# Gated sum of full and sliding-window attention: single PSUM banks in the first and last stage, another load order

## The chip, the core and the metric

The kernel runs on one core of a Trainium2 chip. The metric is device time in microseconds (us) of one execution. The core's engines have queues of their own and meet at semaphores: TensorE (PE, with its weight loads as PEld), VectorE (DVE), ScalarE (ACT), GpSimd (POOL) and SyncE (SP), which issues most of the DMA transfers. Sums of matmuls are made in PSUM, which has eight banks; a bank holds 512 fp32 numbers for each of 128 partitions.

## What is computed

Two attentions over the same input x (2048 tokens, width 512, 32 heads of 16), mixed by a gate for each token:

```python
g = sigmoid((x * gate_w).sum(-1, keepdims=True))
# A: full attention, every query with all 2048 keys
p = softmax(einsum("bhqd,bhkd->bhqk", q, k) * 16 ** -0.5)
a = (p @ v) @ wo_A
# B: eight keys per query, at distances 0, 2, ..., 14 behind it
logits = einsum("bhsd,bhswd->bhsw", q, k[idx]) * 16 ** -0.5
b = (softmax(logits masked where idx < 0) @ v[idx]) @ wo_B
out = g * a + (1 - g) * b
```

Here q, k and v are x times the parts of `A_wqkv` or `B_wqkv`. All inputs and the output are bf16.

## The kernel before

Full attention is the bulk: 32 heads x 16 key tiles of 128 x 4 query chunks of 512 gives 2048 score blocks of 128 keys x 512 queries. They are worked off in 32 periods, each of four heads and one query chunk. ScalarE takes the exponential of most blocks, two or three to an instruction, straight out of PSUM (`pT <- ring`). Two PSUM rings take turns: `rA` of three banks and `rB` of two (`act_stream`). The other blocks are done by polynomials on VectorE (`dve_unit`) or GpSimd (`pool_unit`), from two single banks `w0` and `w1`. The last bank is `acc`, where the products of probabilities and values are summed. Attention B runs on GpSimd beside all this, and the projections to q, k, v and the output go through `w0` and `w1`.

The order of instructions is not written out by hand. A planner (`Plan`) runs through generators, each a job that yields steps such as ("pe", priority, planned duration, function) or ("dve", ...), and records the instructions engine by engine in the order in which a plan with those durations would start them. `Chained` ties each engine's instructions to that order, so every operation has line 339, that of its helper. The planned figures decide the order alone; at run time each engine works through its queue and waits for the semaphores that the framework puts in. The framework keeps account of PSUM by tile: two instructions that touch the same tile, even in different banks of it, can be made to wait for each other.

The first stage, before the first exponential, is this. SP starts the loads: `wkr` (the first 128 key columns), then x in four blocks `xr` of 512 tokens, then `wqr`, `wv` and the rest (lines 389 to 400). TensorE turns each block round, 128 x 128 at a time (`x_half`), and the two halves of a block are copied from PSUM to `xT` by VectorE and ScalarE. The blocks use the banks of the rings: blocks 0 and 2 a tile `xt` of three banks in `rA`, blocks 1 and 3 one of two in `rB`. `XARR` and `WARR` are the planned arrivals. From `xT` come the first keys (`k_job` with i = 0): four matmuls for each block into a bank, of which VectorE takes the maximum (`kmax_all`) and ScalarE writes the copy with a bias (`kt_all`). `sel_job` makes `kmax` and `selk_all` from the maxima; `q_job` makes the first queries: four matmuls, `absq` on VectorE, one matmul with `selk_all`, and `qt` on VectorE. The stream begins with the matmuls of `qt` and `kt_all` into the first ring.

The last stage begins when the last exponentials have read the rings. `end_banks` takes both rings once more, as tiles `last` of three and two banks, and hands out their five banks as resource "e". `post_job` of the last period copies `acc` to `accS`, transposes it, divides by the row sums (`rden`, then `otok`); `ot_job` transposes the result to `oT`; `final_job` and `direct_job` multiply it by the output weights `awo`, and `bwo` for attention B. Of the last four output tiles two go through VectorE (`osb`) and two through ScalarE (`osc`), each followed by its DMA. Among the matmuls stand others into `acc` with zero weights: filler, which the planner puts where TensorE would be idle (`fill_pass`; into `heat` before the stream).

Of the kernel before, what the change touches and what calls it, by code (L numbers as in the profile page):

```python
# [51 lines left out]
class Plan:  # L52
# [36 lines left out]
    def advance(self, gen, t, val):  # L89
        while True:  # L90
            try:
                req = gen.send(val)
            except StopIteration:
                return
            val = None
            op = req[0]
            if op == "acq":
                self.seq += 1
                self.reqs[req[1]].append((req[2], self.seq, t, gen))
                return  # L100
            if op == "rel":
                self.slots[req[1]].append((t, req[2]))
                if len(req) > 3:
                    self.held["job"] -= 1
                continue
            if op == "set":
                ev = req[1]
                ev.time = t
                ws, ev.waiters = ev.waiters, []
                for g_ in ws:  # L110
                    self.advance(g_[0], max(t, g_[1]), None)
                continue
            if op == "wait":
                ev = req[1]
                if ev.time is None:
                    ev.waiters.append((gen, t))
                    return
                t = max(t, ev.time)
                continue
            if op == "delay":  # L120
                t += req[1]
                continue
            if op == "now":
                val = t
# [45 lines left out]
    def gate(self, need):  # L170

        if need is None:
            return 0.0
        if need == "e":
            return min((x[0] for x in self.slots["e"]), default=None)
        if not self.slots[need] or self.held["job"] >= self.cap_job:
            return None
        return min(x[0] for x in self.slots[need])
# [43 lines left out]
    def run(self):  # L222
        while True:
# [27 lines left out]
            else:  # L251
# [22 lines left out]
                    self.idle_fill(st, 1 + (x[6] is not None))  # L274
                if x[6] is not None:
                    slot = self.take(x[6], st)
                    self.held["job"] += 1
                    more = x[5](slot)
                else:
                    more = x[5]()  # L280
# [12 lines left out]
def kernel(  # L293
# [22 lines left out]
    const = ctx.enter_context(tc.tile_pool(name="const", bufs=1))  # L316
    work = ctx.enter_context(tc.tile_pool(name="work", bufs=2))
    ps = ctx.enter_context(tc.tile_pool(name="ps", bufs=1, space=PSUM))

    prev_inst = {}  # L320
    dep_info = mybir.DependencyInfo(mybir.DependencyClass.NoSync, mybir.DependencyReason.SCHED_ONLY)
# [62 lines left out]

    a_w3 = A_wqkv.rearrange("(c p) n -> p c n", p=128)
    xr = [work.tile([128, 2, TPC, D], BF16, name="xr", tag=tg, bufs=1) for tg in ("prod", "vsh")]
    SP.dma_start(out=wkr[:, :, 0:128], in_=a_w3[:, :, D:D + 128])
    for sc in range(NC):
        SP.dma_start(out=xr[sc // 2][:, sc % 2],
                     in_=x2d[sc * QW:(sc + 1) * QW, :].rearrange("(t p) n -> p t n", p=128))  # L390
    SP.dma_start(out=wqr[:, :, 0:128], in_=a_w3[:, :, 0:128])
    SP.dma_start(out=wv[:], in_=a_w3[:, :, 2 * D:3 * D])
    SP.dma_start(out=wkr[:, :, 128:D], in_=a_w3[:, :, D + 128:2 * D])
# [47 lines left out]
    P.resource("pd", 4)  # L441
    P.resource("none", 0)
    P.resource("e", 0)
    P.resource("prod", 1)
    P.resource("vsh", 1)
    P.resource("ob", 1)
# [16 lines left out]
    THIN = 0.40  # L463
    KRP = 4
    QRP = 3
    XARR = (5.0, 6.9, 8.8, 10.7)
    WARR = (3.4, 11.2)
    GP = 4
    BB = 3
    BR = 1  # L470

    ends = []

    class Bank:
        def __init__(self, kind="w"):
# [2 lines left out]
        def open(self, slot, shape, dtype=FP32):  # L478
            self.slot = slot
            if self.kind == "w":  # L480
                self.t = wtile(slot, shape, dtype)
                return
            t = ends[slot] if dtype == FP32 else ends[slot].bitcast(dtype)[:, 0:QW]
            if len(shape) == 4:
                t = t.rearrange("p (a b c) -> p a b c", a=shape[1], b=shape[2])
            self.t = t

        def close(self):
            return ("rel", self.kind, self.slot, 1)
# [28 lines left out]
    v_left = [NG * NT]  # L518
    final_left = [TPC] * NC

    xts = {}
    ev_xfree = {0: ev_x[0], 1: ev_x[1], 2: Event()}

    def x_job(sc):
        yield ("delay", XARR[sc])
        if sc >= 2:
            yield ("wait", ev_xfree[sc - 2])
        xt = ps.tile([128, 3 - sc % 2, QW], FP32, tag="rA" if sc % 2 == 0 else "rB", bufs=1, name="xt")
        xts[sc] = xt
        left = [2]  # L530
        for hf in range(2):
            yield ("spawn", x_half(sc, hf, xt, left))

    def x_half(sc, hf, xt, left):
        v = xt[:, hf, :].bitcast(BF16).rearrange("p (c t) -> p c t", c=DC)

        def tr():
            P.thin = 0.16
            for tt in range(2):
                for c in range(DC):  # L540
                    PE.transpose(out=v[:, c, tt * 128:(tt + 1) * 128],
                                 in_=xr[sc // 2][:, sc % 2, 2 * hf + tt, c * 128:(c + 1) * 128], identity=ident[:])
        yield ("pe", 0, 0.70, tr)
        dst = xT[:, :, sc * QW + hf * 256:sc * QW + (hf + 1) * 256]
        if hf == 0:
            yield ("dve", 1, 0.62, lambda: V.tensor_copy(out=dst, in_=v))
        else:
            yield ("act", 0, 1.05, lambda: A.copy(out=dst, in_=v))
        left[0] -= 1
        if left[0] == 0:  # L550
            yield ("set", ev_x[sc])

    def w_job():
        yield ("delay", WARR[0])
        yield ("act", -1, 0.45, lambda: w_part(A.copy, wkp, wkr, 0))
        yield ("set", ev_wk)
        yield ("delay", WARR[1] - WARR[0])
        yield ("act", -1, 0.45, lambda: w_part(A.copy, wqp, wqr, 0))
        yield ("set", ev_wq)

    def k_job(i, sc, rel, prio):
        if rel is not None:
            yield ("wait", rel)
        yield ("wait", ev_wk)
        yield ("wait", ev_x[sc])
        w = Bank()
        ring = i == 0 and sc == 2

        def pe(s=None):
            if ring:  # L570
                w.t = xts[sc][:, 2, :]
            else:
                w.open(s, [128, QW])
# [3 lines left out]
        yield ("pe", prio, 4 * MM + SW, pe) + (() if ring else ("w",))  # L577
        k_left[0] -= 1
        if k_left[0] == 0:
            yield ("set", ev_kdone)  # L580
# [2 lines left out]
        def top(src):  # L583
            V.tensor_reduce(out=kmax_all[:, i, sc:sc + 1], in_=src, axis=AX.X, op=ALU.max, apply_absolute_value=True)
        if i == 0:
            left = [2]
            done = Event()
            yield ("spawn", k_top(prio, lambda: top(w.t[:]), left, done))
            yield ("act", 0, 0.60, lambda: A.activation(out=kt, in_=w.t[:], func=ACT.Identity, bias=kbias[:, 0:1]))
            left[0] -= 1  # L590
            if left[0]:
                yield ("wait", done)
        else:
            yield ("dve", prio, VP + 0.06, lambda: V.tensor_scalar(out=kt, in0=w.t[:], scalar1=kbias[:, 0:1],
                                                                  scalar2=None, op0=ALU.add))
        if ring:
            yield ("set", ev_xfree[sc])
        else:
            yield w.close()
        if i:  # L600
            yield ("dve", prio, VP, lambda: top(kt))
        yield ("set", ev_k[i][sc])

    def k_top(prio, fn, left, done):
        yield ("dve", prio, VP, fn)
        left[0] -= 1
        yield ("set", done)

    def sel_job(i, prio):
        for sc in range(NC):  # L610
# [370 lines left out]
    def act_stream():  # L981
        while front[0] < NP:
# [23 lines left out]
            for p_, us in parts:  # L1006
# [189 lines left out]
    def post_job(p):  # L1196
# [7 lines left out]
        yield ("acq", "accS", p)  # L1204
        if p == NP - 1:
            st["s"] = work.tile([128, QW], FP32, name="accS", tag="accS", bufs=2)
            left, done = [2], Event()
            yield ("spawn", k_top(0, lambda: V.tensor_copy(out=st["s"][:, 0:256], in_=acc[:, 0:256]), left, done))
            yield ("act", -1, 0.42, lambda: A.copy(out=st["s"][:, 256:QW], in_=acc[:, 256:QW]))
            left[0] -= 1  # L1210
# [425 lines left out]
    P.run()  # L1636
    if CFG_DEBUG:
        import os
        import pickle
# [41 lines left out]
```

## Time and profile before

| | |
|---|---|
| median of 4 runs | 858.87 us |
| the runs | 857.09, 858.69, 859.05, 864.69 us |
| the profiled execution | 859.46 us |
| its span (first to last instruction) | 857.7 us |
| mean granted TensorE clock | 0.992 |
| first exponential over a ring starts | 18.97 us |
| last exponential ends | 845.69 us |
| last copy of an output tile ends (`osc`) | 854.83 us |
| GpSimd busy | 734.6 us (86% of the span) |

Times within the profile count from the start of the span. The profile is of one execution, and the time outside its span (859.46 - 857.7 = 1.76 us) is not in it. The page gives for each engine the busy time, for each group of like instructions the count and the mean, and it follows the chain of work that ended last back to its start. In a row such as `pT<-ring`, the tile written stands left of the arrow and the tile read right of it. Three stages of the span are to be kept apart: before the first exponential, the stream of exponentials, and behind it.

### The profile page before, as it was taken

What the parts mean: (1) busy time and instruction counts of PE and PEld (TensorE: products, weight loads), DVE (VectorE), ACT (ScalarE), POOL (GpSimd) and SP (SyncE); (2) the same over time, 40 slices, a digit from 0 to 9 for tenths busy, and PEclk for the clock granted to TensorE, in tenths of its full rate; (3) what the DMA queues carried; (4) which work ended last, traced back from release to release, by engine and by line L of the source; (5) the groups of instructions that cost most, each with busy time, mean ns of one, the idle gap of its engine ahead of it and who ended that gap; (6) DMA issues with size and microseconds to landing.
All of it is one profiled execution on the core that took longest, in us unless ns stands there. A gap on an engine that the chain in (4) does not pass through costs nothing.

```text
span 857.7 us, 16082 instructions
## 1 busy us (share of the span) xinstructions
PE 754.5 (88%) x6044; PEld 270.9 (32%) x6044; DVE 748.0 (87%) x1313; ACT 833.2 (97%) x754; POOL 734.6 (86%) x740
## 2 busy tenths in 40 slices
PE   8999999888898898888889899988888999888896
PEld 4333343332333322333333233332332332232332
DVE  4588989899999989989999988899889998999885
ACT  5999999999999999999999999999999999999995
POOL 2586798999899989898999998989999998978970
PEclk9999999999999979999999999999999999999999
DMA  9002133312323232121031304213003203010000
GB/s 295 3 2 71 66 130 111 118 63 75 117 63 117 92 105 69 55 63 50 8 111 32 111 32 135 75 56 112 1 14 117 74 20 124 19 50 7 1 2 26
DMA packets 55711, 59.79 MB, mean 70 GB/s; under 512 B 3648, under 2 KB 52288, under 8 KB 55632
## 3 DMA queue, kind: packets, MB, share of 16 engines
q1 hardware_dynamic: 54816, 58.50, 21.3%
q8 instruction: 47, 0.77, 0.4%
q10 hardware_dynamic: 816, 0.26, 0.1%
q14 instruction: 32, 0.26, 0.1%
HBM read 46.14 MB, written 12.62 MB: 69 GB/s over the span
## 4 chain that ended last, share of the span: by engine, by line
ACT 65%; issue 21%; PE 11%; DVE 2%; DMA 1%; SPq 0%; ACTq 0%
ACT pT L339 64%; PE w L339 3%; PE ring L339 3%; PE acc L339 3%; DVE ta L339 1%; ACT lg L339 1%; PE last L339 1%; DMA xr<-in_A_x_dram 1%; PE xt L339 0%; ACT xT L339 0%; DVE kmax_pk L339 0%; DVE xT L339 0%; DVE kpk L339 0%; DVE pd L339 0%; ACT osc L339 0%
## 5 line engine op out<-in xcount | busy, mean ns | idle before, releaser
L339 ACT ACTIVATE pT<-ring 128x1536 bf16<-128x1536 f32 x722 | 821.9, 1385 | 7.3 <-PE ring L339 3.8
L339 PE MATMUL ring<-qt,kt_all 32*128 32x512 bf16 x1849 | 288.4, 383 | 89.5 <-ACT pT L339 74.7
L339 DVE SCALAR_TENSOR_TENSOR ta<-ta,w 128x512 f32<-128x512 f32 x450 | 301.7, 681 | 6.5
L339 POOL TENSOR_TENSOR prod<-prod 128x512 f32<-128x512 f32 (+1 forms) x208 | 240.3, 1166 | 6.0
L339 PE MATMUL acc<-pT,vp_all 128*17 128x512 bf16 x1804 | 225.8, 385 | 0.1
L339 PEld LDWEIGHTS <-kt_all 32*128 32x128 bf16 x2093 | 111.5, 91 | 331.3 <-issue 315.0
L339 DVE TENSOR_SCALAR ta<-w 128x512 f32<-128x512 uint16 x225 | 153.4, 685 | 40.4 <-PE w L339 37.9
L339 PE MATMUL acc<-ident,z 128*32 128x512 bf16 (+4 forms) x745 | 166.2, 338 | 2.4 <-DVE accS L339 2.0
L339 DVE SCALAR_TENSOR_TENSOR pd<-ta,w 128x512 uint16<-128x512 f32 x225 | 151.5, 677 | 1.8
L339 POOL TENSOR_TENSOR prod<-ksh,qb 128x512 f32<-128x512 bf16 x128 | 145.0, 1156 | 2.4
L339 POOL TENSOR_TENSOR prod<-vsh,lg 128x512 f32<-128x512 bf16 x128 | 136.7, 1099 | 2.5
L339 PE MATMUL w<-qt,kt_all 32*128 32x512 bf16 x244 | 92.5, 385 | 0.2 <-DVE pd L339 0.2
L339 PE MATMUL acc<-pd,vp_all 128*17 128x512 bf16 x244 | 78.8, 381 | 0.0
L339 PEld LDWEIGHTS <-z 128*32 128x32 bf16 x775 | 51.8, 95 | 73.7 <-issue 54.0
L339 POOL TENSOR_TENSOR psc<-psc 128x512 f32<-128x512 f32 x57 | 68.0, 1194 | 4.4
L339 PEld LDWEIGHTS <-vp_all 128*17 128x17 bf16 x2048 | 42.4, 88 | 85.3 <-issue 83.1
L339 POOL TENSOR_SCALAR psc<-psc 128x512 f32<-128x512 uint16 (+1 forms) x38 | 23.5, 618 | 39.9 <-DVE psc L339 32.1
L339 PE MATMUL w<-bw,xT 128*128 128x512 bf16 x192 | 49.6, 381 | 0.4
L339 PEld LDWEIGHTS <-xT 128*128 128x128 bf16 x512 | 30.8, 97 | 29.6 <-issue 16.7
L339 POOL TENSOR_TENSOR lg<-lg,mx 128x256 f32<-128x256 f32 x16 | 10.1, 629 | 25.1 <-DVE mx L339 22.8
L339 DVE CAST kvs<-w 128x512 bf16<-128x512 f32 x32 | 21.8, 682 | 3.8 <-PE w L339 3.7
L339 DVE COPY accS<-acc 128x512 f32<-128x512 f32 (+1 forms) x32 | 21.6, 676 | 2.7 <-ACT accS L339 2.0
(115 smaller groups left out, 493.1 us busy)
## 6 DMA issues: line engine op xcount, KB each, us to landing
ksh<-kv_scr SPq DMA_DIRECT2D x16, 1024.0 KB
vsh<-kv_scr SPq DMA_DIRECT2D x16, 1024.0 KB
kv_scr<-kvs SPq DMA_DIRECT2D x16, 256.0 KB
kt_all<-k_scr SPq DMA_DIRECT2D x6, 512.0 KB
q_scr<-qpk SPq DMA_DIRECT2D x24, 128.0 KB
qt<-q_scr SPq DMA_DIRECT2D x24, 128.0 KB
xr<-in_A_x_dram SPq DMA_DIRECT2D x4, 512.0 KB
out_dram<-osb SPq DMA_DIRECT2D x14, 128.0 KB
```

The costliest lines, as they stand in the source:

```text
L339: return chain_on(self._key, f(*a, **k))
```

## The change

The first and the last stage get PSUM tiles of one bank each. In the first stage a pool `ps0` gives five of them, resource "s", to the transposes of x (half a block each) and to the first key matmuls. When the first ring is wanted, that pool is closed and pools for `rA` and `rB` are opened in its place; when the last exponential has read them both, these are closed and a pool of five single tiles "e" is opened. The loads of x and the first of `wkr` are issued by SP and ScalarE; x block 3 goes in two parts. A table says which engine copies which half of `xT`: VectorE has five halves and ScalarE three. For the first keys the copy is a step behind the maximum, and no longer beside it. In the last `post_job` ScalarE copies the first half of `acc` and VectorE the second. The planned arrivals and some planned durations are other numbers, which shifts the recorded order in the first stage and in the last; `held` counts the "w" banks alone.

```diff
-                if len(req) > 3:
+                if len(req) > 3 and req[1] == "w":
                     self.held["job"] -= 1
...
-        if need == "e":
-            return min((x[0] for x in self.slots["e"]), default=None)
+        if need in ("e", "s"):
+            return min((x[0] for x in self.slots[need]), default=None)
...
-                    self.held["job"] += 1
+                    self.held["job"] += x[6] == "w"
...
+    phase = ExitStack()
+    pools = {"s": phase.enter_context(tc.tile_pool(name="ps0", bufs=1, space=PSUM, reuse_waits="tile"))}
+
+    def next_phase(*names):
+        phase.close()
+        for nm in names:
+            pools[nm] = phase.enter_context(tc.tile_pool(name=f"ps{nm}", bufs=1, space=PSUM, reuse_waits="tile"))
...
-    SP.dma_start(out=wkr[:, :, 0:128], in_=a_w3[:, :, D:D + 128])
-    for sc in range(NC):
-        SP.dma_start(out=xr[sc // 2][:, sc % 2],
-                     in_=x2d[sc * QW:(sc + 1) * QW, :].rearrange("(t p) n -> p t n", p=128))
+    def load_x(t0, n):
+        SP.dma_start(out=xr[t0 // 8][:, t0 // 4 % 2, t0 % 4:t0 % 4 + n],
+                     in_=x2d[t0 * 128:(t0 + n) * 128, :].rearrange("(t p) n -> p t n", p=128))
+    A.dma_start(out=wkr[:, :, 0:128], in_=a_w3[:, :, D:D + 128])
+    load_x(0, 4)
+    load_x(4, 4)
+    load_x(8, 4)
+    load_x(12, 2)
+    load_x(14, 2)
...
+    P.resource("s", 5)
...
-    XARR = (5.0, 6.9, 8.8, 10.7)
-    WARR = (3.4, 11.2)
+    XDVE = ((1, 0), (1, 0), (1, 1), (0, 1))
+    XARR = ((5.8, 5.8), (7.2, 7.2), (8.7, 8.7), (9.4, 10.2))
+    WARR = (4.8, 11.3)
...
-                return
-            t = ends[slot] if dtype == FP32 else ends[slot].bitcast(dtype)[:, 0:QW]
-            if len(shape) == 4:
-                t = t.rearrange("p (a b c) -> p a b c", a=shape[1], b=shape[2])
-            self.t = t
+            else:
+                self.t = pools[self.kind].tile(shape, dtype, tag=f"{self.kind}{slot}", bufs=1, name=f"{self.kind}{slot}")
...
     def x_job(sc):
-        yield ("delay", XARR[sc])
-        if sc >= 2:
-            yield ("wait", ev_xfree[sc - 2])
-        xt = ps.tile([128, 3 - sc % 2, QW], FP32, tag="rA" if sc % 2 == 0 else "rB", bufs=1, name="xt")
-        xts[sc] = xt
         left = [2]
         for hf in range(2):
-            yield ("spawn", x_half(sc, hf, xt, left))
+            yield ("spawn", x_half(sc, hf, left))
...
-        yield ("pe", 0, 0.70, tr)
+        yield ("pe", 0, 0.45, tr, "s")
         dst = xT[:, :, sc * QW + hf * 256:sc * QW + (hf + 1) * 256]
-        if hf == 0:
-            yield ("dve", 1, 0.62, lambda: V.tensor_copy(out=dst, in_=v))
+        if XDVE[sc][hf]:
+            yield ("dve", 1, 0.70, lambda: V.tensor_copy(out=dst, in_=w.t[:]))
         else:
-            yield ("act", 0, 1.05, lambda: A.copy(out=dst, in_=v))
+            yield ("act", 0, 1.02, lambda: A.copy(out=dst, in_=w.t[:]))
+        yield w.close()
...
-        w = Bank()
-        ring = i == 0 and sc == 2
+        w = Bank("s" if i == 0 else "w")
...
         if i == 0:
-            left = [2]
-            done = Event()
-            yield ("spawn", k_top(prio, lambda: top(w.t[:]), left, done))
-            yield ("act", 0, 0.60, lambda: A.activation(out=kt, in_=w.t[:], func=ACT.Identity, bias=kbias[:, 0:1]))
-            left[0] -= 1
-            if left[0]:
-                yield ("wait", done)
+            yield ("dve", prio, VP + 0.09, lambda: top(w.t[:]))
+            yield ("act", 0.5, 0.69, lambda: A.activation(out=kt, in_=w.t[:], func=ACT.Identity, bias=kbias[:, 0:1]))
...
-            ring = ps.tile([128, 3 if k % 2 == 0 else 2, QW], FP32, tag=rname, bufs=1, name="ring")
+            if k == 0:
+                next_phase("rA", "rB")
+            ring = pools[rname].tile([128, 3 if k % 2 == 0 else 2, QW], FP32, tag=rname, bufs=1, name="ring")
...
-        yield ("spawn", end_banks("rA", 3))
-        yield ("spawn", end_banks("rB", 2))
-
-    def end_banks(rname, n):
-
-        yield ("acq", rname, 9)
-        t = ps.tile([128, n, QW], FP32, tag=rname, bufs=1, name="last")
+        yield ("acq", "rA", 9)
+        yield ("acq", "rB", 9)
         now = yield ("now",)
-        for k in range(n):
-            ends.append(t[:, k, :])
-            P.slots["e"].append((now, len(ends) - 1))
+        next_phase("e")
+        P.slots["e"] += [(now, n) for n in range(5)]
...
-            left, done = [2], Event()
-            yield ("spawn", k_top(0, lambda: V.tensor_copy(out=st["s"][:, 0:256], in_=acc[:, 0:256]), left, done))
-            yield ("act", -1, 0.42, lambda: A.copy(out=st["s"][:, 256:QW], in_=acc[:, 256:QW]))
-            left[0] -= 1
-            if left[0]:
-                yield ("wait", done)
+            yield ("act", -1, 0.40, lambda: A.copy(out=st["s"][:, 0:256], in_=acc[:, 0:256]))
+            yield ("dve", 0, 0.42, lambda: V.tensor_copy(out=st["s"][:, 256:QW], in_=acc[:, 256:QW]))
...
-    P.spawn(w_job())
+    P.spawn(w_job(0, wkp, wkr, ev_wk))
+    P.spawn(w_job(1, wqp, wqr, ev_wq))
```

More of the change, by code (lines that the diff above doesn't have):

```diff
@@ L470 @@
     BR = 1
-    ends = []
     class Bank:
@@ L519, with x_half, tr @@
     final_left = [TPC] * NC
-    xts = {}
-    ev_xfree = {0: ev_x[0], 1: ev_x[1], 2: Event()}
     def x_job(sc):
-        yield ("delay", XARR[sc])
-        if sc >= 2:
-            yield ("wait", ev_xfree[sc - 2])
-        xt = ps.tile([128, 3 - sc % 2, QW], FP32, tag="rA" if sc % 2 == 0 else "rB", bufs=1, name="xt")
-        xts[sc] = xt
         left = [2]
         for hf in range(2):
-            yield ("spawn", x_half(sc, hf, xt, left))
-    def x_half(sc, hf, xt, left):
-        v = xt[:, hf, :].bitcast(BF16).rearrange("p (c t) -> p c t", c=DC)
-        def tr():
+            yield ("spawn", x_half(sc, hf, left))
+    def x_half(sc, hf, left):
+        yield ("delay", XARR[sc][hf])
+        w = Bank("s")
+        def tr(s):
             P.thin = 0.16
+            w.open(s, [128, DC, 256], BF16)
             for tt in range(2):
                 for c in range(DC):
-                    PE.transpose(out=v[:, c, tt * 128:(tt + 1) * 128],
+                    PE.transpose(out=w.t[:, c, tt * 128:(tt + 1) * 128],
                                  in_=xr[sc // 2][:, sc % 2, 2 * hf + tt, c * 128:(c + 1) * 128], identity=ident[:])
-        yield ("pe", 0, 0.70, tr)
+        yield ("pe", 0, 0.45, tr, "s")
         dst = xT[:, :, sc * QW + hf * 256:sc * QW + (hf + 1) * 256]
-        if hf == 0:
-            yield ("dve", 1, 0.62, lambda: V.tensor_copy(out=dst, in_=v))
-        else:
-            yield ("act", 0, 1.05, lambda: A.copy(out=dst, in_=v))
+        if XDVE[sc][hf]:
+            yield ("dve", 1, 0.70, lambda: V.tensor_copy(out=dst, in_=w.t[:]))
+        else:
+            yield ("act", 0, 1.02, lambda: A.copy(out=dst, in_=w.t[:]))
+        yield w.close()
         left[0] -= 1
@@ L551, in x_half, with w_job @@
             yield ("set", ev_x[sc])
[L553 to L559, printed above, removed]
+    def w_job(n, dst, src, ev):
+        yield ("delay", WARR[n])
+        yield ("act", -1, 0.45, lambda: w_part(A.copy, dst, src, 0))
+        yield ("set", ev)
     def k_job(i, sc, rel, prio):
@@ L565, in k_job, with pe @@
         yield ("wait", ev_x[sc])
-        w = Bank()
-        ring = i == 0 and sc == 2
[L569 to L573, printed above, removed]
+        w = Bank("s" if i == 0 else "w")
+        def pe(s):
+            w.open(s, [128, QW])
             for c in range(DC):
@@ L576, in pe @@
                    c == 0, c == DC - 1)
-        yield ("pe", prio, 4 * MM + SW, pe) + (() if ring else ("w",))
+        yield ("pe", prio, 4 * MM + SW, pe, w.kind)
         k_left[0] -= 1
@@ L595, in k_job @@
                                                                   scalar2=None, op0=ALU.add))
[L596 to L599, printed above, removed]
+        yield w.close()
         if i:
@@ L602, in k_job @@
         yield ("set", ev_k[i][sc])
-    def k_top(prio, fn, left, done):
-        yield ("dve", prio, VP, fn)
-        left[0] -= 1
-        yield ("set", done)
     def sel_job(i, prio):
@@ L1206, in post_job @@
             st["s"] = work.tile([128, QW], FP32, name="accS", tag="accS", bufs=2)
-            left, done = [2], Event()
-            yield ("spawn", k_top(0, lambda: V.tensor_copy(out=st["s"][:, 0:256], in_=acc[:, 0:256]), left, done))
-            yield ("act", -1, 0.42, lambda: A.copy(out=st["s"][:, 256:QW], in_=acc[:, 256:QW]))
-            left[0] -= 1
-            if left[0]:
-                yield ("wait", done)
+            yield ("act", -1, 0.40, lambda: A.copy(out=st["s"][:, 0:256], in_=acc[:, 0:256]))
+            yield ("dve", 0, 0.42, lambda: V.tensor_copy(out=st["s"][:, 256:QW], in_=acc[:, 256:QW]))
         else:
@@ L1636 @@
     P.run()
+    phase.close()
     if CFG_DEBUG:
```

## The prediction

> **What bounds the kernel now.** I read the page's busy table and its costliest group first, then the chain that ended last at both ends of the span, and last the windows around the one dip in the page's clock row.
>
> ```profile
> PE 754.5 (88%) x6044; PEld 270.9 (32%) x6044; DVE 748.0 (87%) x1313; ACT 833.2 (97%) x754; POOL 734.6 (86%) x740
> L339 ACT ACTIVATE pT<-ring 128x1536 bf16<-128x1536 f32 x722 | 821.9, 1385 | 7.3 <-PE ring L339 3.8
> ```
>
> ScalarE is busy for 97% of the span, and 821.9 us of it are the 722 exponentials over the score rings. They run from 18.97 to 845.69 us. So there are three pieces: 18.97 us before the first exponential, 826.7 us of stream, and 12.0 us behind the last one (857.7 - 845.69). Only 4.8 us of the stream are not exponentials (826.7 - 821.9).
>
> The chain of waits before the stream (start, length, what):
>
> ```profile
> 1.22 4.60 DMA xr<-in_A_x_dram
> ...
> 12.49 1.02 PE xt L339 x4
> 13.52 1.81 PE w L339 x8
> ...
> 15.35 0.69 ACT kt_all L339
> ...
> 16.07 0.70 DVE kmax_all L339
> ```
>
> Look at the last two rows. VectorE's maximum over the fourth key block starts only when ScalarE's copy of the same bank has ended. They are two readers of one bank, one after the other, and the maximum stands second. Earlier in the timeline the order is the other way round and costs as much: ScalarE's first `xT` copy begins at 7.69, after VectorE's copy of the other half of the same `xt` tile (6.97 to 7.66), although it needs other data.
>
> The same chain behind the stream:
>
> ```profile
> 846.86 1.85 PE last L339 x9
> ...
> 848.73 0.18 DVE rden L339
> ...
> 848.96 0.61 PE last L339 x2
> ...
> 849.59 0.43 DVE otok L339
> ...
> 850.07 0.83 PE last L339 x6
> ...
> 850.92 0.43 DVE oT L339
> ...
> 851.40 1.05 PE last L339 x4
> ...
> 852.48 0.70 DVE osb L339
> ...
> 853.20 0.59 ACT osc L339
> ...
> 853.83 0.39 PE last L339
> ...
> 854.25 0.58 ACT osc L339
> ```
>
> Here TensorE and VectorE alternate on a tile named `last`. `rden` starts at 848.73, 0.03 us after a projection matmul into another bank of that tile ends, though its transposes ended at 848.48. `otok` waits for two such matmuls, then two more wait for `otok`, and the second `osc` matmul waits for the first `osc` copy. None of these pairs shares data. They share a tile.
>
> **The change, part by part.** In the changed program's order of instructions, what differs stands before the first ring or behind the last one. The exponentials (722), the polynomial blocks on VectorE and GpSimd, and their order in between are the same, and so are their waits but for the numbering of DMA semaphores. So I give the stream 826.7 us as before, and work out the two ends.
>
> *Start.* The x landings first. Timeline: the first transposes start at 5.86, the second pair at 7.33, both released by a DMA. From the bytes on SP's queue in 0.4 us windows I get when each block's data had moved: 5.1 and 6.5 us for blocks 0 and 1, so 0.75 us from there to the landing. The same count gives 8.0 for block 2, 8.8 for the first half of block 3 and 9.5 for the rest: landings (estimates) at 8.8, 9.5 and 10.3.
>
> [...] Row: SP issues wkr at 0.72 for 0.44 us and the x blocks from 1.22. [...] By the trace the engines are 25 to 40% busy from 2.8 to 3.6 us while the gate vector's 528 tiny packets trickle in, so an earlier issue could fill that, but those packets also move 0.45 us later, behind wkr on ScalarE's queue, into block 0 or 1. Bounds for the landings: 0.5 us earlier, 0.5 us later. I take none. The wkr copy into wkp may then come 1 to 2 us later than 3.95 (it shares with x); it is first needed by a matmul at about 8.2, which covers it. ScalarE's table load slips by one 0.48 us issue, inside its 1.23 us wait for wkr. Splitting x block 3 adds one issue of about 0.5 us on SP; wqr, queued behind it, starts as before, since SP lost the 0.5 us of wkr. wv's issue gains a wait for wkr, which has landed by then; wv is first used after the first ring.
>
> Now the steps with the trace's durations: 8 transposes 0.45 to issue and 0.62 to finish, a VectorE `xT` copy 0.69, a ScalarE one 1.01, four key matmuls 1.02 (0.88 to the next group), maximum 0.69, key copy 0.69.
> - Block 0 at 5.86: VectorE starts half a at 6.52, ScalarE half b at 6.97 (7.69 before), done 7.98. Key block 0 can run at about 8.25 (8.76 before), behind block 1's transposes.
> - Block 2 transposes from 9.1, ends 10.2. VectorE: maximum 0 at 9.3 to 9.97, block 2 copies 10.0 to 11.39. Block 3's second half starts on TensorE when it lands, 10.33, and is copied by VectorE at 11.4 to 12.09. ScalarE: key copy 0 behind its maximum (10.0 to 10.7), block 3 half a to 11.7, wqp to 12.1.
> - TensorE then runs keys 1, 2, 3 and the query: 10.88, 11.76, 12.64, 13.52, ending 14.54. Key 3 needs the copies of 12.09: met. The query needs wqp, 12.1: met by 1.4 us.
> - VectorE: maximum 3 from 13.7 to 14.4, then absq 14.58 to 15.27, kmax, selk to 15.75 (17.25 before), selection matmul to 16.19, qt to 16.98, ring at 17.03, and 0.44 us later (18.53 to 18.97 before) the first exponential at 17.47.
>
> ScalarE's key copies now follow the maxima; the last ends at about 15.1, 2.4 us ahead of that. Without this cover each 0.69 us copy would count. Start: 18.97 - 17.47 = 1.5 us gained; 1.0 to 2.0 with the landings' bounds.
>
> *End.* Take the last exponential's end, 845.69, as fixed.
> - Two projection matmuls stood ahead of the last score-times-value matmuls (845.73 and 846.25). They go behind. [...] acc is done at 846.36, not 846.87: 0.5 gained.
> - accS: ScalarE 846.42 to 846.79, VectorE to 847.25, in this order as before. But six projection matmuls (not four) now stand ahead of its transposes: 846.28 + 6 x 0.22 = 847.60. Transposes to 848.26 (848.48 before); 0.3 of the 0.5 is given back.
> - rden no longer waits for the projection: 848.30; reciprocal; otok 848.78 to 849.20. The five projections between issue by 849.15, just hidden. Otok's transposes 849.25 to 849.64 (850.50 to 850.89 before), oT to 850.10.
> - Last four products: 850.15, 850.37, 850.59, then the remaining pair, the end of which no longer waits for a copy. VectorE 850.57 to 851.94 for two outputs; ScalarE 851.0 to 852.2 for the other two (854.83 before).
> - The last DMA goes as before: 857.7 - 854.83 = 2.9 us behind the last copy.
>
> End: 854.83 - 852.2 = 2.6 us gained.
>
> *Sum.* 1.5 + 2.6 = 4.1 us. Span 857.7 - 4.1 = 853.6; the profiled execution 859.46 - 4.1 = 855.4. That execution is 0.6 us above the median of the runs, 858.87; the forecast is for a median: 858.87 - 4.1 = 854.8, 0.48% less.
>
> **The rivals.**
>
> *Only the end is gained (0.13).* The landings decide the start: TensorE runs without a gap from block 3's landing to the query, so each us that it is late moves the first exponential by one. At 1.5 us late (11.8) the start gains nothing: 858.87 - 2.6 = 856.3. For it: wkr and 528 small packets now share the engines with x, not ahead of it. Against: the bytes ahead of x's end are the same, and the engines move 0.35 MB/us from 4 us on.
>
> *Tiles that stay tied (0.08).* The change doesn't do what it says: single banks still wait for one another, say because two engines reading banks beside each other are held apart. Then only the order at the end is worth something, 0.2 us, and the start perhaps 1: 857.7. Against: the new order lists no VectorE or ScalarE wait for the projection matmuls.
>
> *Clock dips in the stream, slower (0.05).* The price is in the trace (busy of PE, PEld, DVE, ACT, POOL, then the clock):
>
> ```profile
> 305.00:308.00 3.00, 2.89 (x18) 0.71 (x19) 2.50 (x5) 2.88 (x4) 2.86 (x3) 0.50 0.71 209
> 308.00:311.00 3.00, 3.00 (x16) 0.36 (x12) 3.00 (x6) 2.46 (x3) 2.19 (x3) 0.50 1.04 322
> 311.00:314.00 3.00, 3.00 (x18) 1.20 (x17) 0.89 (x2) 2.41 (x3) 2.60 (x3) 0.50 0.65 212
> 314.00:317.00 3.00, 3.00 (x21) 0.89 (x20) 2.69 (x8) 2.86 (x4) 2.58 (x3) 0.81 0.00 0
> ```
>
> TensorE runs at half clock from 305 to 315.2 us, and ScalarE, with 2.76 in the next window, loses 15 - 13.37 = 1.6 us. [...] Against: one dip in 826.7 us, and four runs of before within 2 us but for one of 864.69.
>
> **How the numbers follow.** Both ends gained: 0.74, 854.8, with its own range 852.8 to 856.6 (landings 0.5 each way, one dip more or fewer, 0.4 for hand-over times). The rivals take 856.3, 857.7 and 859.6. For 8 in 10: 852.3 to 857.2. A measurement of this kernel tells about 1% (8.6 us) from no change, so all these cases lie within it. Faster by over 1% (850.3) would need twice the sum: 0.03. Slower by over 1% needs eight dips, or a stall in the stream that I don't see: 0.03. Within: 0.94.
>
> **What would show it.** First exponential near 17.5 us and not behind a key copy; `xT` copies of the two engines overlapping; maxima ahead of key copies; the stretch from the last exponential to the end near 9.4 us, with `rden` released by its own transposes and the last two outputs' copies side by side on VectorE and ScalarE; the stream 826.7 us give or take one dip. It is wrong if the stream's length moves by more than 2 us, if block 3 lands after 11, or if the end keeps alternating.

## The result, and the profile after

| | before | after |
|---|---|---|
| median | 859.8 us (63 runs, 857.09 to 866.68) | 857.44 us (44 runs, 853.86 to 862.85) |
| ratio after to before | | 0.997, 95% interval 0.9959 to 0.9982 |
| the profiled execution, and its span | 859.46, 857.7 us | 858.64, 856.9 us |
| first exponential | 18.97 us | 17.74 us |
| from the last exponential's end to the last `osc` copy's end | 8.66 us | 6.34 us |
| from the last exponential's end to the end of the span | 11.5 us | 9.4 us |

The change is a small gain, 0.3%. It is the sign that was forecast and about 0.6 of the forecast size, and the median lies 0.24 us above the range of 852.3 to 857.2. Two of the page's rows after, and its clock row (tenths of full speed in 40 slices):

```profile
PE 756.3 (88%) x6045; PEld 271.3 (32%) x6045; DVE 749.5 (87%) x1314; ACT 832.1 (97%) x753; POOL 734.6 (86%) x740
PEclk9699999999999999999999999999999999999999
L347 ACT ACTIVATE pT<-ring 128x1536 bf16<-128x1536 f32 x722 | 821.9, 1389 | 9.2 <-PE ring L347 5.9
```

The same 722 exponentials take the same 821.9 us, but ScalarE waits 9.2 us ahead of them (7.3 before). The 6 in the second slice of the clock row, 21 to 43 us, says where to look. Here are the windows of that stretch in the kernel after (start and end, length; busy us and count of PE, PEld, DVE, ACT, POOL; clock; DMA share, GB/s):

```profile
26.00:30.00 4.00, 3.66 (x49) 1.70 (x48) 0.69 (x1) 4.00 (x5) 0.85 (x2) 0.92 0.02 4
30.00:34.00 4.00, 4.00 (x31) 1.12 (x29) 0.69 (x1) 2.89 (x3) 3.75 (x4) 0.50 0.00 0
34.00:38.00 4.00, 4.00 (x34) 1.03 (x33) 2.77 (x5) 2.75 (x5) 3.58 (x6) 0.50 0.00 0
38.00:42.00 4.00, 4.00 (x18) 0.76 (x16) 3.35 (x5) 2.98 (x3) 2.65 (x3) 0.50 0.00 0
42.00:46.00 4.00, 4.00 (x24) 1.14 (x23) 3.17 (x6) 2.96 (x4) 0.00 (x0) 0.87 0.02 4
```

and the same windows before:

```profile
26.00:30.00 4.00, 3.54 (x47) 1.51 (x43) 1.18 (x2) 4.00 (x5) 0.00 (x0) 1.00 0.02 4
30.00:34.00 4.00, 4.00 (x52) 1.72 (x51) 0.91 (x2) 4.00 (x4) 3.44 (x4) 1.00 0.00 0
34.00:38.00 4.00, 3.69 (x43) 1.45 (x42) 3.72 (x8) 4.00 (x6) 3.65 (x5) 1.00 0.00 0
38.00:42.00 4.00, 3.91 (x29) 1.11 (x27) 3.93 (x8) 4.00 (x4) 3.69 (x4) 1.00 0.02 4
42.00:46.00 4.00, 4.00 (x35) 1.14 (x32) 3.92 (x7) 3.88 (x5) 1.33 (x3) 1.00 0.00 0
```

TensorE's granted clock is 0.50 from 29.35 us for 13.65 us. It is then busy without a break and still too slow, and ScalarE falls from 4.00 to less than 3 busy us in each 4. From 26 to 46 us it does 15.58 us of work, against 19.88 before: 4.3 us less. The profiled execution before had the one such stretch of its stream elsewhere, from 304.91 us for 10.24 us. Line the two streams up, exponential by exponential, each counted from its first: up to 29 us they agree to 0.02 us. Then the kernel after falls 4.8 us behind within its stretch, keeps that distance to 0.03 us up to 305 us, and gets 2.3 us of it back where the kernel before has its own. From 330 us to the end nothing more changes.

*The start after*, in the chain of waits (start, length, what):

```profile
3.28 7.52 DMA xr<-in_A_x_dram
...
10.85 3.21 PE s L347 x20
14.06 0.88 PE w L347 x4
...
14.96 0.69 DVE absq L347
...
15.75 0.26 DVE selk_all L347
...
17.74 2.37 ACT pT L347 x2
```

`kmax_all` and `kt_all` are gone from the chain: `absq`, not the last maximum behind ScalarE's copy, is what `selk_all` waits for. TensorE goes from block 3's transposes through three key groups to the query without a break. Block 3's second half, though, begins at 10.84, where 10.33 was forecast. Block 3's transposes end at 11.47 us (12.43 before), and the first exponential comes 6.27 us behind them (6.54 before): 0.96 us of the start's gain lies ahead of that point and 0.27 behind it.

*The end.* First the timeline before, for a point that I had read wrongly (start, length, then engine, line, operation):

```profile
837.35 8.82 ACT L339 ACTIVATE pT<-ring 128x1536 bf16<-128x1536 f32 x8
```

The last exponential, of one bank, ends at 837.35 + 8.82 = 846.17 us. The 845.69 of the table of before and of the prediction is where the chain of waits turns to TensorE: the end of the one before it. After:

```profile
838.59 8.82 ACT L347 ACTIVATE pT<-ring 128x1536 bf16<-128x1536 f32 x8
...
847.47 0.58 PE L347 MATMUL acc<-pd,vp_all 128*17 128x512 bf16 x2
...
849.29 0.60 PE L347 MATMUL e<-identf,accS 128*128 128x128 f32 x4
...
849.93 0.17 DVE L347 TENSOR_TENSOR rden<-e,d 128x16 f32<-128x16 f32 x1 [0.97 <-PE e L347]
...
850.42 0.42 DVE L347 TENSOR_TENSOR otok<-e,rden 128x256 bf16<-128x256 f32 x1
...
851.34 0.42 DVE L347 COPY oT<-e 128x512 bf16<-128x512 bf16 x1 [0.49 <-PE e L347]
...
852.25 1.29 DVE L347 TENSOR_TENSOR osb<-e,fpart 128x512 bf16<-128x512 f32 x2 [0.48 <-PE e L347]
...
852.68 1.07 ACT L347 CAST osc<-e 128x512 bf16<-128x512 f32 x2 [4.18 <-PE e L347]
```

The last exponential ends at 847.41, acc is done 0.64 us later, `rden` starts 0.04 us behind its own transposes (849.89), `otok` waits for no matmul, and the two `osc` copies follow each other beside VectorE's two `osb`. The alternation is gone.

Taken together, from these two executions: start 18.97 - 17.74 = 1.23 us, end 11.51 - 9.44 = 2.07 us (with the spans to the hundredth, 857.68 and 856.85), 3.3 us gained outside the stream. The stream took 827.2 us before (18.97 to 846.17) and 829.7 after (17.74 to 847.41), 2.5 us back. So the change's own part shows, and most of it is hidden in this pair by the two half-clock stretches (4.8 and 2.3 us), in a stream whose instructions were not changed.

### The profile page after: what moved, and what is told of

Same layout as the page of the kernel before. It is cut to its first block, busy times and chain, and to the rows that moved or that the text cites. A ratio compares the mean times of both kernels' runs of the same rounds, so it can differ in the third digit from the quotient of the medians.

```text
span 856.9 us, 16085 instructions
## 1 busy us (share of the span) xinstructions
PE 756.3 (88%) x6045; PEld 271.3 (32%) x6045; DVE 749.5 (87%) x1314; ACT 832.1 (97%) x753; POOL 734.6 (86%) x740
## 4 chain that ended last, share of the span: by engine, by line
ACT 66%; issue 21%; PE 9%; DVE 2%; DMA 1%; SPq 0%; ACTq 0%
ACT pT L347 65%; PE w L347 3%; PE ring L347 3%; PE acc L347 3%; ACT lg L347 1%; DVE ta L347 1%; DMA xr<-in_A_x_dram 1%; PE e L347 0%; PE s L347 0%; SPq L347 0%; DVE kmax_pk L347 0%; DVE absq L347 0%; DVE kpk L347 0%; DVE pd L347 0%; DVE crow L347 0%
## 5 line engine op out<-in xcount | busy, mean ns | idle before, releaser
L347 ACT ACTIVATE pT<-ring 128x1536 bf16<-128x1536 f32 x722 | 821.9, 1389 | 9.2 <-PE ring L347 5.9
```

What stands on the lines that cost most here:

```text
L347: return chain_on(self._key, f(*a, **k))
```

## Experiments

Two theories for the stream. **L** (luck): half-clock stretches are drawn anew in each execution, alike in both kernels, and blur a gain of 3.3 us or more. **E** (early): the earlier start draws them in, so that they are a cost of the change. A third, **G**, is about the start: the gate vector's load, put behind `wkr` on ScalarE's queue, slows x.

### Both kernels again, and each end of the change alone

`start_only` is the kernel after with the end of the kernel before, `end_only` the reverse. All instructions between are the same in the four. The edit of `start_only`:

```diff
-        yield ("acq", "rA", 9)
-        yield ("acq", "rB", 9)
-        now = yield ("now",)
-        next_phase("e")
-        P.slots["e"] += [(now, n) for n in range(5)]
+        yield ("spawn", end_banks("rA", 3))
+        yield ("spawn", end_banks("rB", 2))
...
+        t = pools[rname].tile([128, n, QW], FP32, tag=rname, bufs=1, name="last")
```

with `Bank` and the copies of `acc` as before; `end_only` has the removed lines put in the kernel before, with the pools that they need.

> The kernel before, unchanged. All theories: first exponential at 19.0 us, 12.0 us from the last exponential to the end. [...]

> The changed kernel, unchanged. First exponential at 17.7, 9.5 us behind the last one, so 3.7 us less outside the stream than before. Theory L: the median, too, is 3.7 us less than that of the kernel before measured beside it, about 0.996. Theory E: about 2.3 us less, with a half-clock stretch between 25 and 45 us in the profile again and a lower mean clock than the kernel before.

> The first stage of the changed kernel, the last stage of the kernel before. First exponential at 17.7, 12.0 us behind the last. Theory L: median 1.2 us less than before (0.9986). Theory E: no gain or a loss (0 to 1.5 us more), since the stretches of half clock come with the start.

> The last stage of the changed kernel, the first stage of the kernel before. First exponential at 19.0, 9.5 us behind the last. Both theories: median 2.5 us less than before (0.9971). If it is much less, the gain at the end isn't there in most executions and neither theory holds.

| | median (runs) | ratio to before beside it | first exponential | last exponential to last `osc` end |
|---|---|---|---|---|
| same_before | 861.78 (12) | 0.9989 (0.9965 to 1.0012) | 19.34 | 8.66 |
| same_after | 858.73 (12) | 0.9952 (0.9926 to 0.9978) | 17.77 | 6.34 |
| start_only | 857.29 (12) | 0.9961 (0.9937 to 0.9985) | 17.77 | 8.66 |
| end_only | 858.09 (11) | 0.9958 (0.9939 to 0.9977) | 18.95 | 6.34 |

The last two columns repeat to 0.03 us and are additive, but for the start before (18.95 to 19.34), which follows TensorE's warm-up: in all three profiles with the old start the first exponential comes 13.1 us behind the first transposes. (The 12.0 us of the expectations counts from 845.69; from the true end it is 11.5.) The medians are not additive: each end alone seems to gain as much as both, and the ratio of `start_only` lies below what either theory gave it. Half-clock time decides this. Each execution comes with its mean granted clock, and the time follows it:

```text
granted clock (+-0.001)   before, mean us (runs)   after, mean us (runs)
0.997                     858.50 (14)              854.80 (6)
0.993                     859.68 (17)              856.59 (13)
0.990                     861.86 (16)              858.49 (23)
all                       861.33 (86)              857.89 (56)
mean granted clock        0.9907                   0.9908
straight line             856.95 + 0.47 per 0.001  853.26 + 0.50 per 0.001
```

(before: the 12 runs of `same_before` and the runs of the kernel before made beside all timed experiments; after: the 44 first ones and `same_after`.) At equal clock the kernels are 3.1 to 3.7 us apart, and the lines' ends at full clock 3.7. Each end alone is additive in this measure: held to the line of the kernel before at their own mean clocks (0.9924 and 0.9928), `start_only` gains 1.9 us in the mean and `end_only` 2.1, the whole change 3.4. A dozen runs sample the clock badly: six of the twelve of `start_only` lie within 0.06 us of one another, at 0.995, and its median is one of them.

The mean clock is the same in both kernels, and `start_only`, which has the new start, has no lower one than the kernel before beside it (0.9924 against 0.9903). So theory E is not supported as an explanation of the median. L fits: the mean execution of either loses some 4.5 us to half clock (0.0092 x 0.47 to 0.50 per 0.001), more than the change gains, and the two profiles that I compared happened to differ by 2.5. One gap remains. The 63 first runs of the kernel before have no clock on record. On its line their mean, 860.34, would belong to 0.9928, against the 0.9909 of the 44 runs of the kernel after beside them. So in that comparison the kernel after may have had more half-clock time, worth some 0.9 us (an estimate from the line), and why is open.

What E said of the place is not refuted. `after` has its stretch from 29.35 to 43.0 us, and `same_after` has one there, too: its clock is 0.94 from 26 to 30 us, 0.50 from 30 to 42 and 0.86 from 42 to 46. `before` has 1.00 in all of these windows. Whether the new start makes this one stretch more frequent, and another less, would take many profiles of each.

### Filling TensorE so that the clock holds

That half clock comes where TensorE has little to do was a guess of mine, and is not shown: in the 4 us ahead of the stretch of `after` (25.35 to 29.35) TensorE is busy for 3.54 us with 49 matmuls, and in the same 4 us of the stream of `before` (26.60 to 30.60) for 3.54 us with 49, too, with no half clock behind them. To try it I raised the planner's threshold for filler, in both kernels.

```diff
-    THIN = 0.40
+    THIN = 0.55
```

> The kernel before with one planner constant raised (THIN 0.40 to 0.55), so that more zero-weight matmuls go where TensorE's streaming share of the last 3.4 us falls under 0.55. [...]

> The changed kernel with the same constant. Theory L: clock 0.997 or more, runs close together near 853.5 to 854.5, and 3.6 us (3.2 to 4.0) below the filled kernel before in the median: the gain of both ends, whole. Theory E (the earlier start draws in half-clock stretches, so that the gain is truly 2.4): no more than 2.6 us below it. No stretch at 29 us.

> The changed kernel with the constant at 0.60: 16% more filler than unchanged. Theory L: no stretch in the stream at all; 853.5 to 855, where anything above 854 is the price of TensorE's time for the filler. If filler delays the rings more than it keeps the clock: above 856.

> The changed kernel with the constant at 0.55 and gaps of TensorE filled up to a share of 0.85 (0.70 before). Theory L: as the filled changed kernel, 853.5 to 855. If filling gaps costs the riders on VectorE their place: above 856.

Medians: before_filled 872.19 (6 runs), after_filled 871.18 (6), after_filled_more 872.94 (5), after_filled_share 864.41 (12). The three filled kernels after miss the times that theory L gave; the last two expectations had said above 856 for filler that costs time. The clock was held only in `after_filled_more`: 0.998 to 1.000 in its five runs, 872.7 to 874.0, so its 16% more filler costs 19 us over the 853.3 of the kernel after at full clock. `after_filled_share` has 0.996 in the median and costs 9 us at full clock. These kernels are planned anew from the first extra filler on, so that the price holds for the new order and the filler together. The pair of filled kernels differs by 1.0 us with half-clock time in both: it does not tell L from E.

The last try puts the higher threshold in the first 45 us alone:

```diff
-                        and P.have(P.now + dur) < THIN * P.HAM):
+                        and P.have(P.now + dur) < (0.55 if P.now < 45.0 else THIN) * P.HAM):
```

> The changed kernel with the filler constant at 0.55 for the first 45 us of the plan alone, where both profiles of it had a half-clock stretch of 13.7 us that cost 5. The order behind that point shifts a little. Theory L: no stretch near 29 us, the cluster of runs near 858.7 gone, runs without stretches at 853.5 to 854.5, median 855.5 to 857.5 against 857.4 to 858.7 unchanged. If the filler costs as much as the stretch: 858 or more.

861.0 us (12 runs), ratio to before 1.0003 (0.9982 to 1.0024). A stretch of 13.65 us is gone from its profile: a mean clock of 0.997 over 859.2 us leaves some 5 us at 0.50 (an estimate, 2 x 0.003 x 859.2). But `key_back_3` (0.996) and `gate_last_3` (0.993), with the unchanged filler, have no room for it, either (7 and 12 us). The median clock is 0.9975, and five runs at full clock lie at 859.6 to 860.0. So the clock is better and the floor 6 us worse, as the expectation had it for filler that costs as much as the stretch. Half-clock stretches are cheaper than this way of avoiding them.

### What orders the maxima and the copies

`copies_beside` lets the planner put the first key copies where it did before:

```diff
-            yield ("dve", prio, VP + 0.09, lambda: top(w.t[:]))
-            yield ("act", 0.5, 0.69, lambda: A.activation(out=kt, in_=w.t[:], func=ACT.Identity, bias=kbias[:, 0:1]))
+            left = [2]
+            done = Event()
+            yield ("spawn", k_top(prio, lambda: top(w.t[:]), left, done))
+            yield ("act", 0, 0.60, lambda: A.activation(out=kt, in_=w.t[:], func=ACT.Identity, bias=kbias[:, 0:1]))
...
```

> The changed kernel, with each first key copy free to stand ahead of its maximum, as before. In the recorded order the maxima of the last two blocks then wait for ScalarE's copies. First exponential 0.4 to 0.8 us later than 17.7 (18.1 to 18.5) if that order carries the gain of the start; 17.6 to 17.8 if the single banks alone carry it.

One run, 860.49 us; first exponential 18.60. In its timeline two maxima stand together behind ScalarE:

```profile
13.34 1.84 ACT L347 ACTIVATE kt_all<-s,kbias 128x512 bf16<-128x512 f32 x3 [0.75 <-DVE kmax_all L347]
...
14.64 1.29 DVE L347 TENSOR_REDUCE kmax_all<-s 128x1 f32<-128x512 f32 x2 [1.33 <-ACT kt_all L347]
```

VectorE idles 1.33 us until ScalarE's copies let it in: the wait that the chain of before ended in, back again with single banks. TensorE's first transposes were late in this run, too (6.28 us). So count from the end of block 3's transposes: the first exponential comes 6.89 us behind it here (11.71 to 18.60), and 6.27 us in `after` and in the six runs of the next section. By this one run 0.6 us is the order's, within the 0.4 to 0.8 that was expected; 18.5 was passed by 0.1 for the late start.

### Whose packets delay x

The DMA answers for 5.6 to 6.4 us, after and then before (packets, volume; by queue: packets, MB, share of 16 engines):

```profile
DMA packets 391, 0.14 MB, mean 177 GB/s; under 512 B 253, under 2 KB 391, under 8 KB 391
...
q1 hardware_dynamic: 150, 0.14, 53.3%
q10 hardware_dynamic: 241, 0.00, 17.8%
```

```profile
DMA packets 272, 0.27 MB, mean 343 GB/s; under 512 B 4, under 2 KB 272, under 8 KB 272
...
q1 hardware_dynamic: 272, 0.27, 115.7%
```

q10 is ScalarE's queue. Its 241 packets here are the gate vector's, 2 bytes each. While they run, from 5.2 to 7.5 us, x gets half of its pace (177 GB/s against 343); the same program without them (`gate_load_last` below) moves 350 GB/s from 5 to 6 us and 342 from 6 to 7, where `after` has 287 and 125. Before, they ran at 2.4 to 4.0 us, when little else did (112 GB/s in all). Two edits: the gate vector's load last, on SP; or `wkr` back on SP ahead of x, with the gate vector first on ScalarE's queue.

```diff
-        A.dma_start(out=gw[:], in_=gate_w.rearrange("(c p) -> p c", p=128))
...
+        SP.dma_start(out=gw[:], in_=gate_w.rearrange("(c p) -> p c", p=128))
```

```diff
-    A.dma_start(out=wkr[:, :, 0:128], in_=a_w3[:, :, D:D + 128])
+    SP.dma_start(out=wkr[:, :, 0:128], in_=a_w3[:, :, D:D + 128])
```

> The changed kernel, with the gate vector's load issued by SP behind all other loads. Theory G (its 512 packets of 2 bytes, now in the middle of x, halve the transfers from 5.6 to 7.2 us): the last x packets end near 9.4 us, not 10.3; the transposes of block 3 start at 10.0, not 10.8; first exponential at 16.9 (16.7 to 17.1), not 17.7; all else the same, so 0.8 us off the time at equal clock. Rival (x's pace is set by the bytes alone): first exponential at 17.6 to 17.8.

> The changed kernel, with the first key weights' load back on SP ahead of x and the gate vector first on ScalarE's queue, as before. Theory G: the 2-byte packets go by from 2.5 to 4 us again, while the engines have little else; x ends at 9.8 and the first exponential starts at 17.2 (17.0 to 17.4): the load on two queues cost 0.5 us. If it brought its 0.5 us of issue time: 18.2.

The first run of the former missed: first exponential at 18.09. Its timeline says why:

```profile
1.44 4.91 PE L347 MATMUL heat<-ident,z 128*32 128x512 bf16 x12 [1.44 <-DVE wkp L347]
...
6.28 1.46 PE L347 MATMUL s<-ident,xr 128*128 128x128 bf16 x16
```

TensorE's twelve warm-up matmuls, one each 0.43 us, occupy it until 6.28, and the first transposes take 1.46 us instead of 1.07, though x is there. In the kernel after they ended in time for transposes at 5.91. Here they stand 0.43 us apart to the last: their weight loads come at 4.38, 4.81, 5.24 and 5.66. In `after` the spacing turns from 0.43 to 0.22 us at 5.46 us, where the trace's clock record begins, and in `before` it turns at 4.54, where that record begins: up to that point the matmuls take twice the time, as at half clock. The warm-up, no row of my chain, is a bound of the first stage. Further runs of both edits:

> The gate vector's load last, a second look at the start. In the first look the warm-up matmuls ended late (transposes from 6.28, at half clock), so the landings did not decide. If the first transposes start before 6.0 here: first exponential at 17.3 to 17.5 if the earlier x counts (theory G, held to what TensorE's queue leaves of it), 17.7 to 17.8 if it doesn't.

> As the second look at the gate vector's load last: 17.3 to 17.5 where the first transposes start before 6.0 (theory G), about 18.1 where they start at 6.2 or later, as in the first look.

> The first key load back on SP, a second look. Theory G: block 2 and 3 transposes without a gap (1.96 us for 32) and the first exponential at 17.4 to 17.5 again, 0.3 less than with two queues. Else 17.7 or more.

> As the second look at the key load back on SP: 17.4 to 17.5 by theory G.

| | first transposes | blocks 2 and 3 (32 transposes) take | first exponential |
|---|---|---|---|
| after | 5.91 | 2.21 | 17.74 |
| same_after | 5.97 | 2.18 | 17.77 |
| start_only | 5.34 | 2.18 | 17.77 |
| gate_last_2 | 5.87 | 1.95 | 17.29 |
| key_load_back | 5.99 | 1.96 | 17.47 |
| key_back_2 | 6.28 | 1.95 | 17.69 |
| key_back_3 | 6.29, slow (16 in 1.28 us) | 1.95 | 17.91 |
| gate_load_last, gate_last_3 | 6.28, slow (16 in 1.46, 1.48 us) | 1.95 | 18.09, 18.11 |

Where x no longer has a gap (1.95), the first exponential comes 11.4 us behind the first transposes (17.29 - 5.87, 17.47 - 5.99, 17.69 - 6.28), and 0.2 to 0.4 later where the first 16 took 1.28 to 1.48 us and not 1.07. After, with transposes at 5.91, it came 11.83 behind them, and in `start_only` transposes that began 0.6 us earlier still brought nothing: there x is the bound. So in `after` the gate packets cost about 0.4 us. G was right in kind and not in size: the 0.8 us of late x is not all seen, since TensorE's queue is the next bound. Of the two repeats with `wkr` back, neither had 17.4 to 17.5: both started late. The load on two queues did bring x forward where the gate vector was out of the way: from 2 to 7 us `gate_load_last` moves 1.52 MB and `key_load_back` 1.31 (sums of windows of 1 us). The first exponential did not see it, for in both programs TensorE's transposes had no gap (1.95 and 1.96 us for 32). One edit more would keep the gate vector out of x's way, but 0.4 us can't be told in the medians: 858.43 for `gate_load_last` (12 runs; ratio to before 0.997, 0.9949 to 0.9991).

## Why the prediction was wrong, point by point

- *"I give the stream 826.7 us as before"* and *"the forecast is for a median: 858.87 - 4.1"*: this is the step that failed. The miss of 2.7 us (857.44 against 854.8) has three parts. The level was that of four runs, and the median of 63 is 859.8: 0.9 us. The two ends gave 3.3 us in the profiles and not 4.1: 0.8 us (below). The rest, 0.9 us, is the medians' difference of 2.4 us against the stages' 3.3. By the line it is half-clock time that the two sets of runs did not share alike; since the 63 have no clock on record, that is not shown. I took one stretch of half clock for the usual lot, kept it for the kernel after, and spread the range by "one dip more or fewer". On the line of the kernel before, 858.87 belongs to a granted clock of 0.996, where its mean is 0.991; 86 more runs have a mean of 861.3. The kernel after without any is at 853.3 by its line, so its median of 857.44 contains about 4 us of it. A range for a median had to rest on how the times spread with the clock, which one trace can't show. The stream's instructions did take the same time: but for the two stretches the profiles' streams agree to some hundredths. The prediction's own sign of being wrong, a stream that moves by more than 2 us, was met by the two profiles (2.5). At equal clock the forecast of the difference, 4.1, compares with 3.1 to 3.7.
- *The slower rival* had the right mechanism, and its price was too low: "loses 15 - 13.37 = 1.6 us". Lined up with the kernel after, which has no stretch at that place, the same stretch cost 2.3 us, and the one of 13.65 us near 29 us cost 4.8. So one price doesn't serve for every place. The rival's 859.6 is 854.8 and three more dips at 1.6 us, a term that no run shows: the profile after has one stretch in its stream, as the one before, and the twelve runs of `same_after` have mean clocks from 0.981 to 0.997.
- *"Take the last exponential's end, 845.69"*: wrong by 0.48 us, as shown. With it fell the gain of *"acc is done at 846.36, not 846.87"*: acc must wait for 846.17 in either kernel, and was done 0.64 us behind the last exponential after and 0.70 before. The distances of the later steps from that start were right: `rden` 2.52 us behind it (2.61 forecast from 845.69), `otok` 3.01 (3.09), `oT` 3.93 (3.99), the last `osc` end 6.34 (6.5). The gain there was 8.66 - 6.34 = 2.3, not 2.6. What follows the last copy took back 0.25: the span ends 3.10 us behind it, where the forecast kept 2.9 (2.85 before). So "near 9.4 us" from the last exponential to the end came true by luck (9.44): the forecast took 2.6 off 12.0, the runs 2.1 off 11.5.
- *Start*: 1.23 where 1.5 was forecast, within 1.0 to 2.0. The order of maxima and copies, the overlapping `xT` copies and the run of TensorE from block 3 to the query came as worked out. The term that was off is *"Bounds for the landings: ... I take none"*: block 3 was 0.5 late, by the packets that I had named and left at nothing. The first block landed 0.5 us earlier at least, the whole of the earlier bound (its transposes start at 5.34 in `start_only`, at 5.86 before). x came forward in `gate_load_last`, with `wkr` alone on the second queue (1.52 MB from 2 to 7 us, against 1.31 in `key_load_back`), and in `after` the gate vector's packets took that back.
- *"wv's issue gains a wait for wkr, which has landed by then"*: it had not. SP stood still from 4.40 to 5.42 us, since `wkr` landed at about 5.4. It cost nothing: `wv` is used at 17.8 us.

The rival of the tied tiles is refuted by the end's timeline. No run has the single tiles of the last stage with its old order, so how the 2.3 us divide between the two is open. That only the end gains is refuted by 17.74.

## What to carry to other kernels

Compare a small change at equal clock, or by the stages that it touches: here the last stage repeats to some hundredths of a us and the first to 0.4 us, while the total moves by 9. Read the end of the work that bounds a kernel from its own rows, not from the step at which the chain of waits leaves it. When a load moves to another queue, what stands behind it there moves as well, and very small packets can be dear where large ones are in flight (here 177 GB/s instead of 343).

## What the runs showed of the hardware

- The profiled streams each had one stretch at a granted clock of 0.50: 13.65 us long from 29.35 us (`after`), which cost 4.8 us, and 10.24 us long from 304.91 us (`before`), which cost 2.3 us. Over all executions with a clock on record, 0.001 less of mean clock went with 0.47 us more (before) and 0.50 us more (after).
- At the start the windows of the profile show a clock of 1.00 from the first us, though the trace's clock record begins only at 4.54 us (`before`) and 5.46 us (`after`). Until then the 512-column warm-up matmuls stand 0.43 us apart, twice the 0.22 of later ones. The first transposes behind them started between 5.34 us (`start_only`) and 6.29 us (`key_back_3`), and the first exponential moved by 0.8 us where x was not the bound (17.29 in `gate_last_2`, 18.11 in `gate_last_3`).
- The gate vector's 512 packets of 2 bytes on a second queue held the x transfers to 177 GB/s from 5.6 to 6.4 us; without them 343 were moved in this window (`before`), and 350 and 342 from 5 to 6 and from 6 to 7 us (`gate_load_last`).
